# Attention over eight gathered key blocks per query block, in a kernel of block-sparse attention and a gated feed-forward

## The chip, the cores and the metric

One core of a Trainium2 chip runs the kernel. The metric is the time of one execution on the device in microseconds. The kernel before took 958.56 us (median of 3 runs, 957.12 to 958.99). A difference of about 0.2% is what a measurement of this kernel can tell from none.

## The reference

The inputs are q, k and v of shape 4 x 8 x 768 x 64 (batch, heads, tokens, head width), an array of 24 x 3 drawn block numbers, and two weight matrices in 64-bit floats, 512 x 2048 and 2048 x 512. Tokens form 24 blocks of 32.

```python
scores = 0.125 * q @ k.T                                   # per batch and head, 768 x 768
mask = (abs(blk_i - blk_j) <= 1) | first or last block on either side
for qb in range(24):                                       # and three drawn blocks
    for kb in sampled_blocks[qb]: mask[block qb, block kb] = True
scores = where(mask, scores, -1e9)
attn = exp(scores - rowmax); attn /= sum(attn) + 1e-9
x = (attn @ v), heads side by side                         # 3072 x 512
h = x @ w_in
g = where(h >= 1, h, where(h <= -1, 0, (h + 1)**2 / 4))
out = g @ w_out                                            # 3072 x 512
```

So the first and the last query block see all 24 key blocks. Every other one sees its own block and both neighbours, the first and the last block, and its three drawn ones: at most eight blocks, 256 of 768 keys.

## The kernel before

**Attention** works on all 768 keys, and the mask is laid into the operands. One `visit` is one head of one batch (for the first batch, one head and half of the queries). It computes the scores twice. The first pass (`max_mm`, L390) multiplies the rounded q and k with 24 extra rows that hold the mask, and VectorE takes each query's maximum (`max_red`, L396). Those maxima are turned into a row by TensorE (`max_turn`, L420, or `turn_all`, L407) and become one more operand row. The second pass (`scores`, L449 and L450; L447 for the first two visits, in full float32) gives the transposed scores, keys by queries, as the sum of a rounded product and a correction. ScalarE takes the exponential (`expo`, L456), GpSimd adds the tiles for the denominator (`p_sum`, L466; for the first batch TensorE does this with a matrix of ones, L512), and TensorE multiplies with v in float32 (`values`, L478: two products of 64 columns each, one into the upper and one into the lower half of the output). A float32 product is issued as two instructions. x is split into a rounded part and a rest.

**The feed-forward** (`moe`) takes half a batch, 384 tokens, at a time: 8 halves of 16 steps. A step multiplies 4 x 3 times with the first weights (`l1`, L650 to L652, 384 columns), passes the gate on ScalarE and VectorE (L657, L661, L665, L268, L676), and multiplies 3 x 3 times with the second weights (`l2`, L684 to L686, 512 columns). Rounded parts and rests are separate products, three for each one. The 64-bit weights are turned into these pairs on the chip (`convert`, L240 to L253), in the first two halves; the second ones then lie in a scratch in main memory (`wo_dram`) and are read again in every later half (L633).

**The order.** Every piece of work is put on a list with a time (`at`), the list is sorted and issued. The times come from tables of offsets (`P`, `PW`, `PX`, `PA`, `PM`). The feed-forward of one half runs beside the attention of the next ones. Nearly all transfers go through SyncE's queue.

## Time and profile before

| | before |
|---|---|
| median of the runs shown | 958.56 us |
| lowest and highest run | 957.12 and 958.99 us |
| the profiled execution's span | 956.5 us |
| median run less that span | 2.1 us |
| TensorE busy | 98% of the span |
| VectorE, ScalarE, GpSimd busy | 58%, 55%, 27% |
| matmul instructions | 4938 |
| moved by DMA | 155.74 MB, mean 163 GB/s |

The profile gives the span of one execution, from the first to the last instruction; the execution's own time is given only by that span, so what lies around it is taken as the difference to the median run. Engines run side by side and each executes its own list in order. TensorE's busy time counts overlapping matmuls once; the length of one matmul row is its latency, and what one costs in a row of many is the distance from start to start. PEld is the loading of the stationary operand.

### The profile page before, as it was taken

How to read it: one execution, taken by the hardware profiler on the slowest of the kernel's cores; microseconds unless marked ns; L12 is line 12 of the kernel's file. 1: busy time of each engine (PE TensorE's matmuls, PEld its weight loads, DVE VectorE, ACT ScalarE, POOL GpSimd, SP SyncE). 2: the span in 40 equal slices, each digit the busy share in tenths (PEclk: the TensorE clock that was granted, in tenths of full speed). 3: DMA queues.
4: the chain of work that ended last, by engine and by line, in shares of the span. 5: the costliest groups of instructions: out<-in, count | busy, mean ns of one | idle time of the engine just before them, and what ended most of it. 6: DMA issues, size and time to landing. Idle time of an engine off the chain costs nothing.

```text
span 956.5 us, 13865 instructions
## 1 busy us (share of the span) xinstructions
PE 935.7 (98%) x4938; PEld 764.9 (80%) x4938; DVE 550.0 (58%) x976; ACT 525.6 (55%) x1056; POOL 261.2 (27%) x260
## 2 busy tenths in 40 slices
PE   6899999999999999999999999999999999999998
PEld 4555577788888788888898888889888888899997
DVE  4989899867595666545655455555545443222222
ACT  5788687665765555454554454545455444433433
POOL 3000000354344444333443333334433333000000
PEclk9899899999999999999999999999999999999999
DMA  6756566677565655544445555554446423443443
GB/s 165 210 162 210 172 202 180 215 244 238 179 199 157 181 183 155 177 141 155 144 143 159 162 158 179 158 153 131 147 135 200 129 86 107 162 132 121 155 132 99
DMA packets 56025, 155.74 MB, mean 163 GB/s; under 512 B 9566, under 2 KB 17790, under 8 KB 55956
## 3 DMA queue, kind: packets, MB, share of 16 engines
q1 hardware_dynamic: 55700, 154.36, 53.1%
q8 instruction: 39, 0.64, 0.3%
q10 hardware_dynamic: 256, 0.49, 0.2%
q14 instruction: 30, 0.25, 0.1%
HBM read 110.11 MB, written 16.40 MB: 132 GB/s over the span
## 4 chain that ended last, share of the span: by engine, by line
PE 94%; ACT 3%; DVE 1%; issue 0%; DMA 0%; POOL 0%; ACTq 0%; POOLq 0%
PE po L478 13%; PE oa L684 9%; PE oa L686 9%; PE oa L685 9%; PE hp L650 9%; PE hp L651 8%; PE hp L652 8%; PE pa L390 7%; PE pa L449 6%; PE pa L450 6%; ACT pt L456 1%; PE pa L652 1%; PE pa L651 1%; PE pa L650 1%; PE oa L478 1%; PE pa L512 1%
## 5 line engine op out<-in xcount | busy, mean ns | idle before, releaser
L466 POOL TENSOR_TENSOR acc<-acc,pt 128x384 f32<-128x384 f32 x192 | 202.7, 1057 | 169.1 <-ACT pt L456 167.1
L396 DVE TENSOR_REDUCE mc<-pa 128x1 f32<-128x384 f32 x381 | 202.1, 552 | 55.1 <-PE pa L390 50.7
L456 ACT ACTIVATE pt<-pa 128x384 f32<-128x384 f32 x336 | 163.5, 489 | 94.1 <-PE pa L450 84.0
L665 DVE SCALAR_TENSOR_TENSOR r<-r,hp 128x384 f32<-128x384 f32 x112 | 61.7, 550 | 198.8 <-ACT r L661 198.6
L650 PE MATMUL hp<-x,wi 128*128 128x384 f32 x448 | 155.3, 347 | 0.0
L684 PE MATMUL oa<-w,gh 128*128 128x512 f32 x384 | 151.6, 395 | 0.3 <-ACT gh L268 0.3
L686 PE MATMUL oa<-w,gl 128*128 128x512 f32 x384 | 151.5, 394 | 0.1
L651 PE MATMUL hp<-x,wi 128*128 128x384 f32 x448 | 151.6, 338 | 0.0
L466 POOL TENSOR_TENSOR acc<-pt 128x384 f32<-128x384 f32 x48 | 51.2, 1070 | 366.9 <-ACT pt L456 366.9
L685 PE MATMUL oa<-w,gh 128*128 128x512 f32 x384 | 151.2, 394 | 0.0
L652 PE MATMUL hp<-x,wi 128*128 128x384 f32 x448 | 151.1, 337 | 0.0
L657 ACT ACTIVATE r<-hp,half_c 128x384 f32<-128x384 f32 x112 | 65.1, 582 | 113.1 <-PE hp L652 112.9
L478 PE MATMUL po<-pt,lv 128*64 128x384 f32 x720 | 127.2, 495 | 0.0
L390 PE MATMUL pa<-KA,QA 88*128 88x384 f32 x351 | 117.1, 359 | 2.7 <-ACT QA L268 0.9
L450 PE MATMUL pa<-QB,KB 128*128 128x384 f32 x336 | 114.4, 341 | 0.0
L449 PE MATMUL pa<-QA,KA 102*128 102x384 f32 (+1 forms) x318 | 110.5, 347 | 1.7 <-ACT pt L456 1.0
L676 DVE TENSOR_TENSOR gl<-r,gh 128x384 fp32r<-128x384 f32 x128 | 76.5, 598 | 49.3 <-ACT gh L268 48.3
L268 ACT CAST gh<-r 128x384 fp32r<-128x384 f32 x128 | 65.6, 512 | 66.0 <-DVE r L665 65.9
L478 PEld LDWEIGHTS po<-pt,lv 128*64 128x64 f32 x720 | 60.4, 138 | 50.3 <-issue 41.0
L650 PEld LDWEIGHTS hp<-x,wi 128*128 128x128 f32 x448 | 84.5, 189 | 16.8 <-issue 13.6
L651 PEld LDWEIGHTS hp<-x,wi 128*128 128x128 f32 x448 | 84.6, 189 | 1.7 <-issue 0.6
L686 PEld LDWEIGHTS oa<-w,gl 128*128 128x128 f32 x384 | 72.1, 188 | 16.4 <-DVE gl L676 0.6
(134 smaller groups left out, 1201.0 us busy)
## 6 DMA issues: line engine op xcount, KB each, us to landing
w<-wo_dram SPq DMA_DIRECT2D x112, 512.0 KB, 3.3
qk<-in_qk_t_dram SPq DMA_DIRECT2D x24, 384.0 KB, 3.3
raw<-in_moe_w_in_dram SPq DMA_DIRECT2D x16, 512.0 KB, 4.6
raw<-in_moe_w_out_dram SPq DMA_DIRECT2D x16, 512.0 KB, 3.9
wo_dram<-w SPq DMA_DIRECT2D x16, 512.0 KB, 3.4
lv<-in_v_dram SPq DMA_DIRECT2D x40, 192.0 KB, 2.9
out_dram<-o SPq DMA_DIRECT2D x7, 768.0 KB, 5.6
KA<-qkh SPq DMA_DIRECT2D x24, 192.0 KB, 2.7
```

Source lines behind the costliest of these rows:

```text
L390: nc.tensor.matmul(out=pm[:, 0:HALF], lhsT=QAi[0:KM, t * 128:(t + 1) * 128], rhs=KAi[0:KM, kh * HALF:(kh + 1) * HALF], start=True, stop=True)
L396: nc.vector.reduce_max(out=st["mc"][:, t - t0, kh:kh + 1], in_=st.pop(("pm", t, kh))[:, 0:HALF], axis=AX.X)
L450: nc.tensor.matmul(out=ps[:, 0:HALF], lhsT=st["KB"][:, ks], rhs=st["QB"][:, cs], start=False, stop=True)
L456: nc.scalar.activation(out=p, in_=st.pop(("ps", hf, c))[:, 0:HALF], func=AF.Exp, scale=SCALE)
L466: nc.gpsimd.tensor_tensor(out=own["acc"][:, k], in0=prev, in1=st["p", hf, c], op=ALU.add)
L478: nc.tensor.matmul(out=st["po"][(L, R)[k], 0:HALF], lhsT=lv[k][:, c], rhs=p, start=(c == 0), stop=(c == T - 1))
L650: nc.tensor.matmul(out=hv, lhsT=wi[:, j, 0, fs], rhs=x[:, 0], start=(j == 0), stop=False)
L651: nc.tensor.matmul(out=hv, lhsT=wi[:, j, 0, fs], rhs=x[:, 1], start=False, stop=False)
L652: nc.tensor.matmul(out=hv, lhsT=wi[:, j, 1, fs], rhs=x[:, 0], start=False, stop=(j == NP - 1))
L684: nc.tensor.matmul(out=o, lhsT=gh[:, ts], rhs=w[:, 0], start=(fi == fis[0]), stop=False)
L685: nc.tensor.matmul(out=o, lhsT=gh[:, ts], rhs=w[:, 1], start=False, stop=False)
L686: nc.tensor.matmul(out=o, lhsT=gl[:, ts], rhs=w[:, 0], start=False, stop=(fi == fis[-1]))
```

## The change

The layout of the work is new from end to end; the feed-forward's arithmetic stays.

- **Tiles.** A tile is 128 query rows: two neighbouring query blocks of two batches. For two pairs of batches there are 22 such tiles and 2 special ones (first and last block). Three tiles are a group of the feed-forward, 384 tokens, 8 groups.
- **Gathered keys and values.** For each normal tile and each half of the heads, 8 key blocks for each of two query blocks are copied inside on-chip memory from the whole k (`kt`) into `kg`: three neighbours, three drawn ones at addresses read into registers (`k_random`, always GpSimd), the first and the last. v comes from main memory by DMA in the same way (`v_static`, `v_random`, addresses read by SyncE). A drawn block that is already seen, or drawn twice, is kept in the keys and replaced by a block of zeros in v. v has a column of ones, so the denominator comes out of the same product.
- **Scores once.** They are computed in float32, queries by keys: 16 products for a half tile, each with 64 rows, 32 columns of the array and 256 moving columns. VectorE takes the maximum from PSUM, ScalarE the exponential with it as bias, TensorE turns the result (4 transposes for each of two), ScalarE and VectorE copy it back, and TensorE multiplies with v: 32 products with 32 columns of the array and 65 moving columns. Special tiles take all 768 keys, one head at a time.
- **Order.** `Plan` holds each piece with a duration, a priority, what it needs and what buffers it holds, simulates the engines once with these durations, and issues in the order of the simulated starts. On every engine that order is fixed then.
- **Buffers.** After the first group, attention has PSUM banks 0 to 2, the first layer 3 and 4 (0 to 4 in the last group), the outputs 5 to 7. x of two groups fits on the chip.

The weights are converted in pieces of 128 x 512, 32 times, with the same operations as before. A special tile takes one head at a time: 2 x 4 score products of 384 columns, 2 x 3 transposes, 6 x 4 value products.

```diff
--- before.py
+++ after.py
-    plan.sort(key=lambda x: x[0])
-    for _, fn, args in plan:
-        traced(fn, *args)
...
+    for pair in range(B // 2):
+        units = lambda *blocks: [(2 * pair + k, i) for k in range(2) for i in blocks]
+        normal = [("n", pair, t, units(2 * t + 1, 2 * t + 2)) for t in range(NB // 2 - 1)]
+        special = ("s", pair, None, units(0, NB - 1))
+        tiles += normal[:6] + [special] + normal[6:]
...
+    LATENCY = {"PE": 0.28, "ACT": 0.1, "DVE": 0.1, "POOL": 0.15, "SP": 0.0}
+    DMA_RATE, DMA_WAIT = 260e3, 2.0
...
+                    end = now + dur
+                    done = end + self.LATENCY[name]
+                    if name == "SP" and t["size"]:
+                        dma_free = max(dma_free, end + 0.3) + t["size"] / self.DMA_RATE
+                        done = dma_free + self.DMA_WAIT
+                    e["at"] = end
...
+        placed.sort(key=lambda x: (x[0], x[1]))
...
+        return [t["fn"] for _, _, t in placed]
...
+    def load_k(pair, hh, prio):
+        key = ("kt", pair, hh)
+        add(SP, 0.45, prio, lambda: nc.sync.dma_start(out=new("kt", key).rearrange("p i b j k -> p (i b j k)"), in_=kt_in[pair, :, hh]),
+            give=[key], hold=[("kt", key)], size=128 * 12288)
...
+            def v_static(k):
+                i = units[k][1]
+                vg = new("vg", ("vg", n, k))
...
+                nc.sync.dma_start(out=vg[32 * (lo - i + 1):32 * (hi - i + 1), 0], in_=v_in[pair, lo * BLK:hi * BLK])
+                if globe.get(place) != pair:
+                    globe[place] = pair
+                    nc.sync.dma_start(out=vg[64:96, 1], in_=v_in[pair, 0:BLK])
+                    nc.sync.dma_start(out=vg[96:128, 1], in_=v_in[pair, (NB - 1) * BLK:S])
+            def v_random(k):
+                _, regs = nc.values_load_multi_w_load_instructions(
+                    vix[0:1, 6 * t + 3 * k:6 * t + 3 * k + 3], engines=(SP_ENGINE,), min_val=0, max_val=S,
+                    skip_runtime_bounds_check_because="clamped on the chip to the blocks there are")
+                vg = of(("vg", n, k))
+                for to, r in zip((vg[96:128, 0], vg[0:32, 1], vg[32:64, 1]), regs):
+                    nc.sync.dma_start(out=to, in_=v_in[pair, bass.ds(r, BLK)])
...
+                def k_static(kg=kg, kt=kt):
+                    to = new("kg", kg).rearrange("p i s b c -> p i s (b c)")
+                    eng = nc.vector if n < GT else nc.gpsimd
+                    src = of(kt).rearrange("p i b j k -> p i (b j k)")
+                    for k in range(2):
+                        i = units[k][1]
+                        eng.tensor_copy(out=to[:, k, 0:3], in_=src[:, i - 1:i + 2])
+                    for s, blk in ((6, 0), (7, NB - 1)):
+                        eng.tensor_copy(out=to[:, :, s], in_=src[:, blk:blk + 1].to_broadcast([128, 2, 4 * BLK]))
+                def k_random(kg=kg, kt=kt):
+                    _, regs = nc.values_load_multi_w_load_instructions(
+                        kix[0:1, 6 * t:6 * t + 6], engines=(POOL_ENGINE,), min_val=0, max_val=NB - 1,
+                        skip_runtime_bounds_check_because="clamped on the chip to the blocks there are")
+                    to = of(kg).rearrange("p i s b c -> p i s (b c)")
+                    src = of(kt).rearrange("p i b j k -> p i (b j k)")
+                    for k in range(2):
+                        for r in range(NR):
+                            nc.gpsimd.tensor_copy(out=to[:, k, 3 + r:4 + r], in_=src[:, bass.ds(regs[3 * k + r], 1)])
+                add(DVE if n < GT else POOL, 1.7, prio - 2 + 0.9 * hh, k_static, need=[kt, *kchain], give=[(*kg, "s")], hold=hold)
+                add(POOL, 3.5, prio - 2 + 0.9 * hh + 0.2, k_random, need=["ix", (*kg, "s")], give=[kg], now=[(*kg, "r")], hold=hold)
...
+                kchain[:] = [(*kg, "r")]
...
+                nc.tensor.transpose(out=a[:, j * 128:(j + 1) * 128], in_=of(("xs", n))[:, j * 128:(j + 1) * 128], identity=idf)
...
+        def scores():
+            banks = [new("bank", k) for k in sa]
+            for jj in range(2):
+                for u in range(4):
+                    for e in range(2):
+                        nc.tensor.matmul(out=banks[e][32 * u:32 * u + 32, 256 * jj:256 * jj + 256],
+                                         lhsT=of(q)[rows_of[e], 2 * hh + jj, 32 * u:32 * u + 32],
+                                         rhs=of(("kg", n, hh))[rows_of[e], u % 2, :, u // 2, jj * BLK:(jj + 1) * BLK], start=True, stop=True, skip_group_check=True)
+        def top(e):
+            if e == 0:
+                new("nm", nm)
+            nc.vector.tensor_reduce(out=of(nm)[:, 2 * e:2 * e + 2], in_=of(sa[e]).rearrange("p (j k) -> p j k", j=2), axis=AX.X, op=ALU.max,
+                                    negate=True)
+        def expo(e, jj):
+            if jj == 0:
+                new("p", pk[e])
+            nc.scalar.activation(out=of(pk[e])[:, jj], in_=of(sa[e])[:, 256 * jj:256 * jj + 256], func=AF.Exp,
+                                 bias=of(nm)[:, 2 * e + jj:2 * e + jj + 1])
+        def turn(e):
+            a = new("bank", ta[e])
+            for jj in range(2):
+                for c in range(2):
+                    at = (2 * jj + c) * 128
+                    nc.tensor.transpose(out=a[:, at:at + 128], in_=of(pk[e])[:, jj, c * 128:(c + 1) * 128], identity=idf)
...
+        def values():
+            o = new("bank", ob)
+            for jj in range(2):
+                for e in range(2):
+                    h = 4 * hh + 2 * jj + e
+                    k = 2 * jj + e
+                    for c in range(2):
+                        for u in range(4):
+                            nc.tensor.matmul(out=o[32 * u:32 * u + 32, k * VW:(k + 1) * VW], lhsT=of(tk[e])[:, jj, c, 32 * u:32 * u + 32],
+                                             rhs=of(("vg", n, u % 2))[:, c, u // 2, h * VW:(h + 1) * VW], start=(c == 0), stop=(c == 1),
+                                             skip_group_check=True)
...
+            def scores(e=e, jj=jj, sa=sa):
+                for i in range(2):
+                    bank = new("bank", sa[i])
+                    for u in range(4):
+                        nc.tensor.matmul(out=bank[32 * u:32 * u + 32, 0:384], lhsT=of(q)[rows_of[e], 2 * hh + jj, 32 * u:32 * u + 32],
+                                         rhs=of(kt)[rows_of[e], 12 * i:12 * i + 12, u // 2, jj], start=True, stop=True, skip_group_check=True)
...
+                for c in range(6):
+                    pt = of(tk[c // 3]).rearrange("p j c q -> p (j c) q")
+                    for u in range(4):
+                        nc.tensor.matmul(out=o[32 * u:32 * u + 32, k * VW:(k + 1) * VW], lhsT=pt[:, c % 3, 32 * u:32 * u + 32],
+                                         rhs=of(("vg", n, c // 2))[:, c % 2, u // 2, h * VW:(h + 1) * VW], start=(c == 0), stop=(c == 5),
...
+        add(SP, 0.45, prio - 5, load, give=[("raw", key)], hold=[raw], size=128 * 4096)
+        add(ACT, 0.65, prio, absolute, need=[("raw", key)], give=[("abs", key)], hold=[raw, cva])
+        add(DVE, 2.1, prio, bits, need=[("abs", key)], give=[("bits", key)], hold=[raw, cva])
+        add(ACT, 0.62, prio, hi, need=[("bits", key), *order], give=[("hi", key)], hold=[cva, *hold])
+        add(DVE, 0.75, prio, lo, need=[("hi", key)], give=[key], hold=[cva, *hold])
...
+    for name, g, fis, fresh in (("0l", 0, low, True), ("1l", 1, low, False), ("0h", 0, high, True), ("1h", 1, high, False)):
+        step = STEP_A
+        gated(name, g, fis, t, step, fresh, fis is low, fis is high)
+        if g == 0:
+            for q in sorted({fi // 4 for fi in fis}):
+                for k in range(4):
+                    w_in_part(k, q, 1.5 + 2 * k if q == 0 else t + (4 * q - fis[0]) * step - WI_LEAD + 0.1 * k)
+        t += len(fis) * step
+    for g in range(2, len(GROUPS)):
+        gated(str(g), g, full, t, STEP_B, False, True, True)
...
+        if ring == "bank":
+            moe = isinstance(key[1], str)
+            plan.only[key] = set(range(3 if key[1] < "7" else 0, 5)) if key[0] == "h" else {5, 6, 7} if moe else set(range(8 if key[1] < GT else 3))
...
+    order = plan.order()
+    with tc.manual_schedule():
+        for fn in order:
+            fn()
+T0, T1, MOE0 = 0.0, 22.0, 34.0
+STEP_A, STEP_B, LEAD, WI_LEAD = 6.0, 5.6, 20.0, 8.0
```

## Rows read from the trace of the kernel before

**Rows 1.** The page: busy time of the engines, and the chain that ended last, by line.

```profile
PE 935.7 (98%) x4938; PEld 764.9 (80%) x4938; DVE 550.0 (58%) x976; ACT 525.6 (55%) x1056; POOL 261.2 (27%) x260
...
PE po L478 13%; PE oa L684 9%; PE oa L686 9%; PE oa L685 9%; PE hp L650 9%; PE hp L651 8%; PE hp L652 8%; PE pa L390 7%; PE pa L449 6%; PE pa L450 6%; ACT pt L456 1%; PE pa L652 1%; PE pa L651 1%; PE pa L650 1%; PE oa L478 1%; PE pa L512 1%
```

**Rows 2.** Stretches: PE, PEld, DVE, ACT, POOL busy (instructions), clock, DMA share, GB/s.

```profile
0.00:25.00 25.00, 16.86 (x48) 10.21 (x50) 12.08 (x30) 15.00 (x27) 7.27 (x20) 1.00 0.65 164
25.00:100.00 75.00, 67.98 (x373) 39.84 (x372) 67.71 (x122) 60.45 (x117) 0.00 (x0) 0.92 0.65 194
...
500.00:600.00 100.00, 100.00 (x534) 86.16 (x533) 53.17 (x98) 49.76 (x105) 35.92 (x36) 1.00 0.56 165
```

**Rows 3.** Timeline of TensorE late: first second-layer matmuls of two steps (start, length).

```profile
851.16 0.39 PE L684 MATMUL oa<-w,gh 128*128 128x512 f32 x1
...
855.36 0.39 PE L684 MATMUL oa<-w,gh 128*128 128x512 f32 x1
```

**Rows 4.** Chain in order of time: float32 matmuls, stationary 128, 64 and 32 wide.

```profile
22.82 0.65 PE oa L447 x2
...
30.67 2.09 PE po L478 x12
...
53.34 2.07 PE oa L512 x24
```

**Rows 5.** Timeline of TensorE: three transposes of 128 columns and what follows.

```profile
66.08 0.34 PE L420 MATMUL pa<-idr,mr 128*1 128x128 f32 x3
66.26 0.56 PE L390 MATMUL pa<-KA,QA 88*128 88x384 f32 x2
```

**Rows 6.** Timeline of TensorE: small products (L538), then v products, then first-layer ones.

```profile
502.75 0.24 PE L538 MATMUL pa<-sel,PS 128*64 128x32 f32 x1
502.76 0.54 PE L478 MATMUL po<-pt,lv 128*64 128x384 f32 x1
502.82 0.22 PE L538 MATMUL pa<-sel,PS 128*64 128x32 f32 x1
...
506.88 0.45 PE L650 MATMUL hp<-x,wi 128*128 128x384 f32 x1
507.16 0.34 PE L651 MATMUL hp<-x,wi 128*128 128x384 f32 x1
507.34 0.34 PE L652 MATMUL hp<-x,wi 128*128 128x384 f32 x1
```

**Rows 7.** Groups by line and shape, busy us, mean ns: loading a stationary operand.

```profile
L512 PEld LDWEIGHTS pa<-pt,ones 128*32 128x32 f32 x96 | 2.7, 109 | 5.5 <-issue 4.3 <-ACT gh L268 0.6 <-DVE cva L241 0.6
```

**Rows 8.** The same view: the gate of one feed-forward step, and the running maximum.

```profile
L657 ACT ACTIVATE r<-hp,half_c 128x384 f32<-128x384 f32 x112 | 65.1, 582 | 113.1 <-PE hp L652 112.9
L661 ACT ACTIVATE r<-r 128x384 f32<-128x384 f32 x128 | 66.9, 523 | 1.5
L665 DVE SCALAR_TENSOR_TENSOR r<-r,hp 128x384 f32<-128x384 f32 x112 | 61.7, 550 | 198.8 <-ACT r L661 198.6
L268 ACT CAST gh<-r 128x384 fp32r<-128x384 f32 x128 | 65.6, 512 | 66.0 <-DVE r L665 65.9
L676 DVE TENSOR_TENSOR gl<-r,gh 128x384 fp32r<-128x384 f32 x128 | 76.5, 598 | 49.3 <-ACT gh L268 48.3
L396 DVE TENSOR_REDUCE mc<-pa 128x1 f32<-128x384 f32 x381 | 202.1, 552 | 55.1 <-PE pa L390 50.7
```

**Rows 9.** The same view: conversion of weights on VectorE.

```profile
L241 DVE TENSOR_SCALAR cva<-cva 128x1024 f32<-128x1024 f32 x16 | 11.3, 706 | 1.2 <-ACT cva L240 1.1
L244 DVE SCALAR_TENSOR_TENSOR cva<-raw,cva 128x1024 int32<-128x1024 int32 x16 | 20.2, 1266 | 0.2
L253 DVE TENSOR_TENSOR wi<-cva,wi 128x512 fp32r<-128x512 f32 x16 | 11.2, 709 | 2.4 <-ACT wi L268 2.2
```

**Rows 10.** The same view: GpSimd, one-operand copy.

```profile
L266 POOL TENSOR_SCALAR x<-KB 38x768 fp32r<-38x768 f32 x1 | 0.8, 829 | 0.1
```

**Rows 11.** The page: DMA issues, KB each, us to landing.

```profile
w<-wo_dram SPq DMA_DIRECT2D x112, 512.0 KB, 3.3
```

More of the change, by code (lines that the diff above doesn't have):

```diff
@@ L73, in f @@
+    plan.rings["bank"] = list(range(8))
+    slots = {}
+    for ring, (n, size) in sizes.items():
+        for i in range(n):
+            if (ring, i) not in LENDERS:
+                slots[ring, i] = sb.tile([128, size], types.get(ring, F32), name=f"{ring}{i}")
+    for i in range(8):
+        slots["bank", i] = ps.tile([128, 512], F32, name=f"bank{i}")
+    made, extra, early = {}, {}, {}
     def f(ap):
         return ap.bitcast(F32)
-    idr = cst.tile([128, 128], F32R, name="idr")
-    eps = cst.tile([128, 1], F32, name="eps")
@@ L157, in mask_rest @@
-    def mask_rest():
-        mask_half(1, nc.scalar)
-        for i in range(1, ALL):
-            rounded(nc.gpsimd, QA[i][64:KM, HALF:S], f(QA[0][64:KM, HALF:S]))
-    plan = []
-    passed = set()
-    def after(key, *needs):
-        assert all(x in passed for x in needs), (key, needs)
-        passed.add(key)
-    def at(t, fn, *args):
-        plan.append((t, fn, args))
-    fence = [None, 0]
-    def pe_from(k):
-        return [i for i in nc.cur_bb.bb.instructions[k:] if i.engine == mybir.EngineType.PE]
@@ L177, in behind @@
-    def behind(i, first):
-        tc.add_manual_dep(i, first.name, mybir.DependencyInfo(mybir.DependencyClass.NoSync, mybir.DependencyReason.DATA),
-                          reason="order")
-    def fenced(fn, *args):
-        k = len(nc.cur_bb.bb.instructions)
-        last = pe_from(-200)[-BEFORE:] if BEFORE else []
-        fn(*args)
-        new = pe_from(k)
-        for i in last:
-            behind(new[0], i)
-        for a, b in zip(new, new[1:]):
-            behind(b, a)
-        fence[:] = [new[-1], AFTER]
@@ L192, in traced @@
-    def traced(fn, *args):
-        k = len(nc.cur_bb.bb.instructions)
-        fn(*args)
-        if fence[1] and fn is not fenced:
-            for i in pe_from(k):
-                behind(i, fence[0])
-                fence[1] = max(0, fence[1] - 1)
-    turns = {}
-    def bank(wide, use="s"):
-        if wide:
-            ring = RINGS[use]
-            n = turns[use] = turns.get(use, -1) + 1
-            name = ring[n % len(ring)]
-            if name[0] == "o":
-                return psc.tile([128, DM], F32, name=name)
-            if name == "hp":
-                return psh.tile([128, 512], F32, name="hp")
-        return psa.tile([128, 512], F32, name="pa")
@@ new lines, in body, with load_consts @@
+    vix = cst.tile([1, 66], I32, name="vix")
+    wo_dram = dr.tile([NF, 128, 2 * DM], F32R, name="wo_dram")
+    parts = [dr.tile([GT, 128, DM], F32, name=f"part{i}") for i in range(2)]
+    at_ix = {}
+    def load_consts():
+        o = new("o", ("o", "ix"))[0:1]
+        post, s_f, bad, tmp = (o[:, k * NB * NR:(k + 1) * NB * NR] for k in range(4))
+        sraw = new("raw", ("raw", "ix"))[0:1, 0:NB * NR]
+        at_ix.update(post=post, s_f=s_f, bad=bad, tmp=tmp, sraw=sraw)
+        nc.sync.dma_start(out=sraw, in_=sampled_blocks.bitcast(I32).rearrange("a (r w) -> (a r) w", w=2).unsqueeze(0))
+        nc.sync.dma_start(out=post, in_=pos)
@@ new lines, in first @@
+    def first():
+        nc.scalar.activation(out=warm, in_=half_c, func=AF.Exp)
+    ix = [("o", ("o", "ix")), ("raw", ("raw", "ix"))]
+    add(SP, 0.9, -100, load_consts, give=["sraw"], size=1e3, hold=ix)
+    add(SP, 0.45, -40, load_ident, give=["idf"], size=64e3)
+    add(DVE, 3.2, -100, indices, need=["sraw"], give=["ix"], hold=ix)
+    add(ACT, 1.6, -100, first, need=["ix"], give=["warm"])
+    kchain, globe = [], {}
+    chain = dict(T=[], K=[], V=[])
+    L, R = slice(0, 64), slice(64, 128)
@@ L757, in body @@
+    STEP = 6.1
+    for pair, hh in ((0, 0), (0, 1), (1, 0), (1, 1)):
+        load_k(pair, hh, -50 + hh if pair == 0 else 200 + hh)
+    starts = {0: T0, 1: T1}
+    passes = []
     full = tuple(range(NF))
     low, high = full[:NF // 2], full[NF // 2:]
[L759 to L761 removed]
```

1148 lines of the change are left out of this document (516 added, 632 removed).

## The prediction

> **What bounds the kernel now.** I read the page first: TensorE is busy 98% of the span, the other engines at most 58%, and the chain that ended last is a list of TensorE lines [rows 1]. The stretches say the same by time: from 200 us on TensorE never stops, and only the first 100 us, where VectorE and ScalarE are nearly as full, have gaps [rows 2]. So the span is the sum of TensorE's work plus a ragged start, and a change is worth the TensorE time that it takes away. The chain by line shows which that is: L478, L390, L449 and L450 are attention, L650 to L652 and L684 to L686 the feed-forward. The timeline gives the part that stays: one feed-forward step starts 4.20 us after the one before [rows 3], and 128 steps (8 halves by 16) make 538 us. The other 956.5 - 538 = 418 us of the span are attention, conversion and start. The change can reach only these.
>
> **What small float32 products cost.** The new attention uses float32 products with 32 columns of the array, so their pace decides the sum. A float32 product is two instructions. With a stationary operand 128 wide two follow in 0.65 us, 325 ns each; 64 wide, in two halves of the array, twelve take 2.09 us, 174 ns each; 32 wide, in four quarters, 24 take 2.07 us, 86 ns each, all for 384 columns [rows 4]. So halving the width doubles how many run at once.
>
> - *Scores, half a normal tile:* 16 products of 256 columns. At L512's pace (2.07 us for 12 of 384) that is 1.84 us if only the four quarters run side by side. They use half of the rows of the array, alternately; if the two row halves also run side by side, 0.92. No row shows this. I take 0.92, since each halving in rows 4 doubled the rate, and keep 1.84 as the upper end.
> - *Transposes:* three of 128 columns take 0.18 us, 60 ns each, with rounded operands [rows 5]; a full float32 product of 128 columns would be 650/3 = 217 ns. I take one float32 instruction, 108 ns, since the transpose rows are one instruction each. Eight for a half tile: 0.86 us.
> - *Values, half a normal tile:* 32 products of 65 columns, 64 instructions, 16 in each quarter. By columns one lasts 325 x 65/384 = 55 ns. Loading 32 columns takes 109 ns from start to end [rows 7] and may not hide behind so short a product: upper end 164 ns. L538's two instructions of 32 columns, each with its own load, start 70 ns apart [rows 6]; that is the nearest row, so 16 x 0.07 = 1.12 us.
> - *Change of shape:* after the v products the first full matmul holds TensorE 0.28 us in place of 0.18 [rows 6], 0.1 us a change, four changes a half.
>
> The Trainium skill, page "TensorE: Matmul & The Clock Gate", section "Wait — 56ns, not 53.3ns?", has a rule against this change: starts never come closer than about 25 ns, however short the product. By it 64 value instructions take 1.6 us instead of 1.12. The trace has two starts 0.01 us apart in different halves of the array (502.75 and 502.76 [rows 6]), so it does not agree where products lie beside each other; by the rule the sum below grows by 27 us, to 834.
>
> A normal tile then costs 2 x (0.92 + 0.86 + 1.12 + 0.4) + 0.43 (four more transposes) = 7.0 us, 22 of them 155 us. A head of a special tile: 8 score products of 384 columns 1.38, six transposes 0.65, 48 value instructions 0.84, changes 0.3: 3.2 us; eight heads and 0.43 make 25.8, two tiles 52. Attention falls from 418 us, start included, to 207 us of TensorE; with the feed-forward 745.
>
> **What lies beside it.** For a group of three tiles TensorE needs 67 + 2.75 x 7.0 + 0.25 x 25.8 = 93 us. ScalarE: 16 gates of 0.582 + 0.523 + 0.512 us [rows 8] are 26, attention at the same 0.512 us for 384 columns some 17: 43. VectorE: 16 x (0.550 + 0.598) = 18, and for a tile four maxima over 512 columns (0.552 x 512/384 = 0.74 each [rows 8]), two copies of the same size, and some 2.2 us of scaling and splitting, 6.6 us together: 41 in all with a special tile's share. The old maxima and GpSimd's sums are gone. GpSimd copies 768 columns in 0.829 us [rows 10]; a half tile copies 1280 + 768 columns, 2.2 us, so a tile with its scaling 5 us, and 12 address reads whose cost no row shows: from nothing up to the 3.3 us in which an ordinary load lands [rows 11], which would be 45 us a tile. I take a tenth of that, 0.33 us each, 9 us a tile against 31 us of TensorE for it. SyncE reads 6 addresses a tile, ahead of its transfers; what is queued behind them are the second-layer weights of later steps, one each 5.8 us. All of it is hidden behind TensorE after the start. If the cover is gone, TensorE waits for scores.
>
> **The start.** The feed-forward cannot begin before three tiles are done, and the gather needs whole k first. By the code's sizes 3.1 MB of k, 0.8 of q, 6.1 of v and some 3 of raw weights are queued on SyncE before: 13 MB. DMA moved 164 GB/s at a share of 0.65 in the first 25 us [rows 2], 250 at a full share: 52 us. TensorE does 21 us of attention in it. Then VectorE is late next: the first 8 steps need 12 more weight pieces of (2 x 0.706 + 2 x 1.266)/2 + 0.709 = 2.7 us [rows 9], 32 us, 9 of gates and 20 for the next three tiles, 61 us, against 34 + 21 = 55 of TensorE. The two wait for each other in turn, so I add 15 us, with 6 and 30 as ends.
>
> **The sum.** 52 + (745 - 21) + 15 = 791; 10 us for gaps where a tile comes late in a fixed order (1.4% of the rest; before there were none after 200 us, in the crowded stretch 9%); 4 for the last copy and store: a span of 805 us. The runs' median lies 2.1 us above the profiled span of 956.5, so 807 us.
>
> **Rivals.**
>
> - *TensorE's small products cost more.* If the row halves take turns, +0.92 x 44 = 40 us; if a transpose costs both float32 instructions, 109 ns x 544 = 59. One alone 847 or 866, both 906. For it: no row has 64-row products or float32 transposes. Against: rows 4 for the first. In the other direction, transposes at 60 ns and values at 55 ns would save 39: 768.
> - *The fixed order does not fill TensorE.* It comes from guessed durations, and attention is a chain over three engines with three banks. If TensorE is busy as in 25 to 100 us before, 67.98 of 75 [rows 2], the rest takes 724/0.906 = 799: a time of 857. For it: the stretch in which the old order was short of work. Against: every attention step has feed-forward products to lie beside it.
> - *Starts of small products are spaced* (slower). If each instruction takes 60 ns to start, as the transposes of rows 5 are apart, a half tile's values take 3.84 us and its scores 1.92, a special head's values 2.88: 44 x (2.72 + 1.0) + 16 x 2.04 = 197 us more, 1004. It turns slower than before from a spacing of 51 ns on. Against it: the 0.01 us of rows 6. At the skill's 25 ns it is the 834 above, within my range.
> - *GpSimd's address reads become the bound* (slower). After the start 19 tiles are gathered one after the other; with the last group's 67 us and the 52 and 4 us that takes 125 + 19 x (5 + 12r), longer than before from r = 3.2 us on; at 3.3, about 972. Against: a read from memory on the core should not last as long as a 512 KB load.
>
> **How the numbers follow.** Forecast 0.55 (its own range 768 to 835); the 25 ns rule 0.06; costlier products 0.14; order 0.13; spaced starts 0.04; address reads 0.06; within 0.2% 0.02 (0.2% is what a measurement tells from no change). Faster 0.88, same 0.02, slower 0.10. The range 750 to 890 leaves out both slower cases, no change, and the costlier products where both hold and a little of the order.
>
> **What would show it.** Right: matmul instructions for attention in runs of 32 within 0.9 to 1.0 us and of 64 within 1.0 to 1.2; transposes about 0.11 us apart; feed-forward steps still 4.2 us of TensorE; the first first-layer product near 52 us; TensorE full from some 110 us on. Wrong: scores over 1.5 us a half, float32 transposes as pairs, GpSimd busy or waiting for registers most of the span, TensorE below 95% in the middle with a wait for VectorE, ScalarE or GpSimd in front of scores, or a start much longer than 52 us.

## The result, and the profile after

The changed kernel takes 812.04 us (median of 4 runs, 811.55 to 813.06); the kernel before took 958.77 beside it. The ratio is 0.848, 95% interval 0.8464 to 0.8496: 147 us less. The profiled execution took 811.55 us with a span of 809.8. The forecast was 807 us, its span 805.

The page after, busy time by engine and the chain by line; these answer to [rows 1]:

```profile
PE 755.9 (93%) x8480; PEld 623.3 (77%) x8480; DVE 406.7 (50%) x830; ACT 380.5 (47%) x768; POOL 154.5 (19%) x441
...
PE 85%; DMA 10%; DVE 2%; SPq 1%; ACT 1%; issue 1%; ACTq 0%
PE bank L673 11%; PE bank L708 11%; PE bank L675 11%; PE bank L710 11%; PE bank L674 11%; PE bank L709 10%; DMA vg<-in_vx_dram 5%; PE bank L487 5%; PE bank L449 4%; PE bank L470 4%; PE bank L530 3%; DMA raw<-in_moe_w_out_dram 2%; DMA early_wi<-in_vx_dram 2%; PE bank L565 2%; PE bank L548 1%; PE bank L398 1%
```

TensorE still sets the time, but it is no longer full from end to end: its work fell by 180 us (935.7 to 755.9), the span by only 146.7, so some 33 us more than before pass with TensorE idle. The feed-forward lines L673 to L675 and L708 to L710 fill 65% of the span; the attention lines L449 (scores), L470 (transposes) and L487 (values), with L530 to L565 for the special tiles, some 19%. DMA stands in the chain with 10%, and it had no line there before. The stretches say where (columns as in [rows 2], so that the last three are the granted clock, the DMA share and GB/s):

```profile
0.00:25.00 25.00, 4.33 (x42) 2.42 (x42) 14.34 (x44) 7.42 (x13) 5.66 (x22) 1.00 0.93 299
25.00:50.00 25.00, 17.03 (x386) 10.27 (x386) 17.91 (x44) 11.07 (x23) 4.79 (x13) 0.96 1.05 253
50.00:75.00 25.00, 13.85 (x254) 9.11 (x252) 19.10 (x37) 11.09 (x23) 14.50 (x38) 0.70 0.99 275
75.00:100.00 25.00, 24.33 (x467) 19.52 (x468) 23.00 (x45) 17.28 (x35) 15.86 (x35) 1.00 0.80 247
500.00:600.00 100.00, 100.00 (x1075) 80.92 (x1074) 39.15 (x82) 41.88 (x84) 7.58 (x22) 1.00 0.42 146
600.00:700.00 100.00, 95.88 (x1219) 78.17 (x1218) 41.95 (x87) 47.16 (x98) 27.16 (x82) 0.98 0.60 171
```

TensorE works 35 of the first 75 us, 24.33 of the next 25, and then nearly all. No engine is full in the first 75 us; the DMA share is (0.93 to 1.05). Between 50 and 75 us, with TensorE half idle, the granted clock is 0.70: part of the stretch at the lower of the two levels.

The small products, from the chain of waits in order of time (start, length, what); of the kernel before, [rows 4 and 5] are the nearest:

```profile
386.10 1.02 PE bank L449 x32
387.13 1.05 PE bank L487 x64
388.17 0.37 PE bank L673
389.42 0.87 PE bank L470 x8
```

A half normal tile takes 1.02 us for scores, 1.05 for values and 0.87 for eight transposes, which are one instruction each (x8); the first full matmul behind the values holds 0.37.

The timeline of TensorE: the first first-layer matmul, the first of the second pass, and two second-layer starts late, which answer to [rows 3]:

```profile
73.07 0.67 PE L673 MATMUL bank<-xh,wi 128*128 128x384 f32 x1
...
123.56 0.33 PE L673 MATMUL bank<-xh,wi 128*128 128x384 f32 x1
...
740.28 0.39 PE L708 MATMUL bank<-w,gh 128*128 128x512 f32 x1
...
744.47 0.39 PE L708 MATMUL bank<-w,gh 128*128 128x512 f32 x1
```

A step still takes 4.19 us. The feed-forward starts at 73.07 us, not at 52; its first eight steps last 50.5 us, not 70; from there to the end are 686.2 us, where the forecast's terms give 683. So the total hit because a start that was forecast 21 us too short and a stretch behind it that was forecast 20 us too long cancelled.

### The profile page after: what moved, and what is told of

Same layout as the page of the kernel before. It is cut to its first block, busy times and chain, and to the rows that moved or that the text cites. A ratio compares the mean times of both kernels' runs of the same rounds, so it can differ in the third digit from the quotient of the medians.

```text
span 809.8 us, 20914 instructions
## 1 busy us (share of the span) xinstructions
PE 755.9 (93%) x8480; PEld 623.3 (77%) x8480; DVE 406.7 (50%) x830; ACT 380.5 (47%) x768; POOL 154.5 (19%) x441
## 4 chain that ended last, share of the span: by engine, by line
PE 85%; DMA 10%; DVE 2%; SPq 1%; ACT 1%; issue 1%; ACTq 0%
PE bank L673 11%; PE bank L708 11%; PE bank L675 11%; PE bank L710 11%; PE bank L674 11%; PE bank L709 10%; DMA vg<-in_vx_dram 5%; PE bank L487 5%; PE bank L449 4%; PE bank L470 4%; PE bank L530 3%; DMA raw<-in_moe_w_out_dram 2%; DMA early_wi<-in_vx_dram 2%; PE bank L565 2%; PE bank L548 1%; PE bank L398 1%
## 5 line engine op out<-in xcount | busy, mean ns | idle before, releaser
L673 PE MATMUL bank<-xh,wi 128*128 128x384 f32 x512 | 181.6, 355 | 0.0
L675 PE MATMUL bank<-xh,wi 128*128 128x384 f32 x512 | 173.1, 338 | 0.3 <-DVE wi L616 0.3
L674 PE MATMUL bank<-xl,wi 128*128 128x384 f32 x512 | 172.3, 336 | 0.0
L708 PE MATMUL bank<-w,gh 128*128 128x512 f32 x384 | 157.3, 410 | 0.3 <-ACT gh L589 0.3
L678 ACT ACTIVATE r<-bank,half_c 128x384 f32<-128x384 f32 x128 | 74.5, 582 | 173.6 <-PE bank L675 172.9
L710 PE MATMUL bank<-w,gl 128*128 128x512 f32 x384 | 152.5, 397 | 1.8 <-DVE gl L690 1.8
L709 PE MATMUL bank<-w,gh 128*128 128x512 f32 x384 | 151.5, 395 | 0.0
L673 PEld LDWEIGHTS bank<-xh,wi 128*128 128x128 f32 x512 | 96.5, 189 | 15.6 <-issue 9.7
L674 PEld LDWEIGHTS bank<-xl,wi 128*128 128x128 f32 x512 | 96.6, 189 | 3.9
L675 PEld LDWEIGHTS bank<-xh,wi 128*128 128x128 f32 x512 | 96.2, 188 | 0.9 <-DVE wi L616 0.9
L708 PEld LDWEIGHTS bank<-w,gh 128*128 128x128 f32 x384 | 72.3, 188 | 19.2 <-issue 3.1
L710 PEld LDWEIGHTS bank<-w,gl 128*128 128x128 f32 x384 | 72.3, 188 | 18.8 <-DVE gl L690 2.8
L379 POOL COPY kg<-kt 128x128 f32 x264 | 75.9, 334 | 32.2 <-PE bank L449 15.8
L709 PEld LDWEIGHTS bank<-w,gh 128*128 128x128 f32 x384 | 72.4, 189 | 10.6
L449 PE MATMUL bank<-kg,q 64*32 64x256 f32 x1408 | 53.6, 407 | 16.1 <-POOL kg L379 15.5
```

What stands on the lines that cost most here:

```text
L379: nc.gpsimd.tensor_copy(out=to[:, k, 3 + r:4 + r], in_=src[:, bass.ds(regs[3 * k + r], 1)])
L449: nc.tensor.matmul(out=banks[e][32 * u:32 * u + 32, 256 * jj:256 * jj + 256], lhsT=of(q)[rows_of[e], 2 * hh + jj, 32 * u:32 * u + 32], rhs ...
L673: nc.tensor.matmul(out=hv, lhsT=wi[:, j, 0, fs], rhs=xh, start=(j == 0), stop=False)
L674: nc.tensor.matmul(out=hv, lhsT=wi[:, j, 0, fs], rhs=xl, start=False, stop=False)
L675: nc.tensor.matmul(out=hv, lhsT=wi[:, j, 1, fs], rhs=xh, start=False, stop=(j == 3))
L678: nc.scalar.activation(out=new("r", rk[1]), in_=of(hk[1])[:, 0:TOK], func=AF.Relu, bias=half_c, scale=0.5)
```

## The experiments

Four runs test the prices of the new attention, one what the gather is worth, six the start. Ratios are against the kernel before, with the 95% interval.

**The scores in the two row halves of the array.** Every product reads the same 64 rows; as many of each kind as before.

```
-                for u in range(4):
-                    for e in range(2):
-   lhsT=of(q)[rows_of[e], ...], rhs=of(("kg", n, hh))[rows_of[e], ...]
+                for e in range(2):
+                    for u in range(4):
+   lhsT=of(q)[rows_of[0], ...], rhs=of(("kg", n, hh))[rows_of[0], ...]
```

> The scores of a normal half tile take both factors from the lower 64 rows of the array for both heads of a pair (so half of the scores are computed from the wrong head), four quarters after one another; nothing else changes. If the two row halves run side by side in the changed kernel, as forecast, a half tile's 16 score products go from 1.02 us to about 1.9, and 44 halves cost some 40 us: 850. Rival: the row halves take turns already and the low price comes from elsewhere: no change, 812.

839.47 us, ratio 0.8763 (0.8739 to 0.8788). The chain of waits:

```profile
391.49 1.86 PE bank L449 x32
```

1.86 us is the upper end that the prediction had kept (1.84), and 1.02 is near the one it took (0.92): products in the two row halves run side by side. The time rose by 27 us and not by all 44 x 0.84 = 37; where the rest went is shown with the third run.

**Values in the order of the quarters.** Four instructions in a row go to one quarter of the columns; before, neighbours went to different quarters.

```
-                    for c in range(2):
-                        for u in range(4):
+                    for u in range(4):
+                        for c in range(2):
```

> The same value products in another order: both halves of the keys of one query block follow each other, so four instructions in a row go to the same quarter of the array. If products run side by side only when neighbours in the list go to different quarters, a half tile's 64 value instructions go from 1.04 us to between 2.6 (48 of 64 steps of 55 ns) and 3.5 (all 64), and the kernel to between 880 and 920. Rival: TensorE finds work for a free quarter by itself: 812.

815.94 us, ratio 0.8503 (0.847 to 0.8535), hardly apart from the change's own. The chain of waits:

```profile
391.90 1.11 PE bank L487 x60
```

I had expected 2.6 to 3.5 us a half; it is 1.11 in place of 1.05. That expectation took TensorE to start its list strictly in order, and it fell: the quarters still work side by side when four neighbours of the list share one. Whether the engine starts later products first or hands them to a queue in each quarter the trace doesn't tell. The Trainium skill, page "TensorE: Matmul & The Clock Gate", section "The mechanism", has weight loads pulled ahead but matmuls in strict order of start and end; by the second half of that rule the 2.6 us should have stood, and 1.11 speaks against it.

**The price of a transpose.** Every block of four is done twice, eight more a half, with the same result.

```
-            for jj in range(2):
+            for jj in (0, 1, 0, 1):
```

> Each transpose of the exponentials in normal tiles is issued twice into the same place. At 0.109 us each that is 8 x 0.109 = 0.87 us more TensorE work in a half tile, 38 us in 44 halves. Theory (TensorE is the bound from the first feed-forward product on, and a transpose costs one float32 instruction): 850, less some 5 for halves that lie in the uncovered start. Rival: part of its busy time is slack that a fixed order leaves: under 830.

842.34 us, ratio 0.8791 (0.8768 to 0.8814). The chain of waits:

```profile
358.97 1.75 PE bank L470 x16
```

Sixteen take 1.75 us, 109 ns each; the prediction's 108. A group of three normal tiles grew by 5.2 us (88 to 93 from the first product of one to that of the next), which is 6 x 0.87: there TensorE alone sets the time. But the pass from 533.2 to 649.9 us, which has a special tile beside it, stayed at 116.6 here and in the first run. It is the pass of the middle in which the work comes late most: the stretch from 600 to 700 us above has 95.88 busy, and in it TensorE waits for gathered values (1.22 and 1.01 us at 625 and 627 us) and for exponentials (1.42). The first 123.6 us likewise took only 6.4 of the 10.4 us added there. Extra work of TensorE is paid where it is full and free where it is not.

**The address reads.** All reads of block numbers into registers are replaced by fixed numbers; as many copies and transfers as before.

```
-                _, regs = nc.values_load_multi_w_load_instructions(vix[...], engines=(SP_ENGINE,), ...)
+                regs = [(3 + (5 * t + 7 * r + k) % 18) * BLK for r in range(NR)]
-                    _, regs = nc.values_load_multi_w_load_instructions(kix[...], engines=(POOL_ENGINE,), ...)
+                    regs = [3 + (5 * t + 7 * r + r // 3) % 18 for r in range(2 * NR)]
```

> The drawn blocks are taken from addresses fixed when the kernel is built (other blocks than the reference draws); the copies and transfers stay in number and size, only the reads of addresses into registers go. Theory: they are hidden everywhere, 812 within 2. Rival: SyncE's reads hold up the first values, for which TensorE waits until 24 us, and GpSimd's the first scores: 3 to 6 us less. Second rival, address reads as a bound: 20 us less or more.

812.01 us, ratio 0.8479 (0.8453 to 0.8505): no change. In the trace of the changed kernel, the reads of addresses (six each on GpSimd, three each on SyncE) and GpSimd's gathered copies by kind (count: ns shortest/median/longest, first and last start):

```profile
L372 POOLq TENSOR_LOAD <-kix x44: 774/888/3001, 5.0 to 697.2; - x44
L343 SPq TENSOR_LOAD <-vix x44: 662/673/1151, 16.8 to 703.4; - x44
L379 POOLq FUSED_REGOPS  x264: 46/46/58, 6.0 to 699.0; - x132
L379 POOL COPY kg<-kt x264: 287/293/783, 7.6 to 700.2; 128x128 f32 x132
```

Reading six addresses takes GpSimd 0.89 us (median), 0.15 each; at every copy comes a register operation of 46 ns. Together that is some 0.19 us an address, against the 0.33 us that I took and the 3.3 at the upper end [rows 11]. GpSimd is busy 19% of the span. The rival of the address reads needed 3.2 us each and is out by a factor of some sixteen.

**All keys for all heads.** The gather is left out: every tile goes the way of the special ones, with 12 blocks of keys in place of eight.

```
-        if kind == "n":
+        if False:
```

> Every tile goes the way of the special ones: no gather, all 24 key blocks, one head at a time (unmasked, so the output is that of full attention). It tells what the gather is worth inside the new layout. TensorE's sum by the pieces measured in the changed kernel (per head 1.42 for scores, 0.66 for transposes, 0.82 for values and some 0.3 for changes of shape: 26 us a tile): 538 + 24 x 26 = 1162, with start and end above 1200, slower than the 958 of the kernel before. Rival: the layout (scores once, the denominator from a column of ones, no second pass) is what pays and the gather adds little: under 900. The chain of one head through three engines with three banks may not keep TensorE full: then up to 1500.

1512.76 us, ratio 1.5779 (1.5717 to 1.5841), at a clock of 0.86. The page, then the chain of waits over one head:

```profile
PE 1336.7 (88%) x16224; PEld 919.1 (61%) x16224; DVE 630.9 (42%) x1378; ACT 551.4 (36%) x1076; POOL 13.5 (1%) x25
```

```profile
701.10 0.59 ACT p L542
701.74 1.54 PE bank L548 x6
703.28 1.27 PE bank L565 x48
704.55 0.82 PE bank L530 x8
...
705.46 0.56 DVE nm L536
706.04 0.57 DVE nm L536
706.63 0.17 DVE nm L538
...
706.91 0.59 ACT p L542
```

One head follows the other: scores, maximum, exponential, transposes, values, 5.81 us from one exponential to the next, of which TensorE has 3.6; through the maximum and the exponential only feed-forward products can fill it. 22 normal tiles at the special tile's 26 us in place of 7 would be some 413 us more, 1225; the measured 1513 is beyond that, with the chain over three engines and the lower clock on top. By the page TensorE is busy 1336.7 us, 175 more than the expected sum of 1162, which the clock of 0.86 would about make (1162/0.86 = 1351, an estimate), and idle for another 175 of the span of 1511.9. So the two are of about one size, and even the sum of 1162 alone is above the 958 before: within this layout it is the gather on the chip, not the planned order alone, that makes the kernel faster.

**What the start waits for.** In the first 73 us, what made the engines wait in the changed kernel (us in total, times, longest):

```profile
PE bank L449 <- POOL kg L379: 15.5, 2, 13.0
PE bank L470 <- ACT p L462: 9.5, 4, 6.3
...
ACT p L462 <- DVE nm L456: 10.3, 3, 6.7
ACT q L315 <- DMA q<-in_qt_dram: 10.0, 1, 10.0
ACT cva L602 <- DMA raw<-in_moe_w_out_dram: 6.8, 3, 5.3
...
POOL q L317 <- DMA q<-in_qt_dram: 18.5, 2, 13.9
```

TensorE waits for gathered keys and for exponentials; GpSimd and ScalarE, which make these, wait for loads. Two theories: the *bytes* bind (the GB/s of the three stretches above make 20.7 MB by 75 us; the forecast counted 13 before the first product), or the *order* does, since an engine that works its list in order stands in front of an instruction whose load hasn't landed, with ready work behind it. A third is VectorE, which converts weights beside attention.

The first run on this loads only half the partitions of each raw weight, which takes away 8.4 MB in all, about half of it before 123.6 us:

```
-            nc.sync.dma_start(out=new("raw", ("raw", key)), in_=src...)
+            raw = new("raw", ("raw", key))
+            nc.sync.dma_start(out=raw[0:64], in_=src[0:64]...)
...
+    for i in range(3):
+        nc.gpsimd.memset(slots["raw", i][64:128].bitcast(F32), 1.0)
```

> Only the upper 64 of 128 rows of each 64-bit weight piece are transferred (the other rows hold ones, so half of the weights are wrong); everything else stays. 32 x 0.26 MB less, 4.2 MB of it before the second pass of the feed-forward begins at 123.6 us. If DMA bounds the first 120 us (at shares of 0.93 to 1.05 until 75 us, some 275 GB/s): 15 us less, 797. If VectorE and the order of work bound them: 0 to 3 us less.

811.29 us, ratio 0.8467 (0.8435 to 0.85): nothing to be told from no change. The stretch from 50 to 75 us, then the time up to the first first-layer product in the changed kernel and in this run, and the landing of the halved loads (KB each, median us):

```profile
50.00:75.00 25.00, 15.61 (x270) 10.70 (x262) 20.83 (x41) 11.24 (x23) 14.54 (x37) 0.64 0.97 252
```

```profile
0.00:73.10 73.10, 33.31 (x673) 19.99 (x673) 49.65 (x121) 28.63 (x58) 24.95 (x72) 0.90 0.99 274
```

```profile
0.00:71.30 71.30, 34.51 (x672) 21.63 (x673) 50.67 (x121) 28.80 (x58) 28.09 (x75) 0.87 0.98 250
...
raw<-in_moe_w_in_dram SPq DMA_DIRECT2D x16, 256.0 KB, 5.1
raw<-in_moe_w_out_dram SPq DMA_DIRECT2D x16, 256.0 KB, 4.0
```

TensorE is nearly as idle as before. Up to the first product 17.8 MB move (71.3 us at 250 GB/s) in place of 20.0; at the changed kernel's rate the difference is worth 8 us, and the product comes 1.8 us earlier. So the number of these bytes does not set the start. But the DMA share stays at 0.97 though fewer bytes move in it (252 GB/s in place of 275), and a half load still takes 5.1 and 4.0 us to land where a whole one took 6.5 and 5.0. So the share does not go by bytes, and whether the time of the transfers binds, rather than their bytes, this run does not tell.

The second takes two of the five VectorE instructions off each piece of weights:

```
-            nc.vector.tensor_scalar(out=f(a), in0=f(a), scalar1=CLO, scalar2=CHI, op0=ALU.max, op1=ALU.min)
-            nc.vector.scalar_tensor_tensor(out=a, in0=raw[:, :, 1], scalar=-0x40000000, in1=a, ...)
```

> Two of the four bit operations with which VectorE converts a weight piece are left out (clamp and sign, so the weights are wrong); their 0.44 and 0.70 us go, 1.14 x 32 = 37 us of VectorE's time, 18 us of it before 123.6 us. If VectorE bounds the first 120 us: 10 to 18 us less, 794 to 802. If DMA bounds them, the conversion waits for its load all the same: 0 to 3 us less.

804.88 us, ratio 0.8406 (0.8376 to 0.8435), between the two expectations. VectorE has some 16 us less to do before the second pass; the second pass starts 2.7 us earlier (120.9), the end comes 8 us earlier in the profile, 3.1 of them from the third pass (39.1 us in place of 42.2), where weights are still converted. So VectorE is a part of it, and before the second pass a small one.

Both at once (the two diffs above together):

> Half of each raw weight piece is transferred and two of the four bit operations are left out, both at once (the weights are wrong). If transfers and VectorE each cover for the other in the first 120 us, together they give far more than the 1 and 7 us one by one: 15 us less or more, under 797. If order and latency bind them: not much more than the sum, 802 to 805.

806.29 us, ratio 0.8435 (0.8408 to 0.8462): no more than the second alone, so the bytes of the raw weights weren't hidden behind VectorE either.

The order, first in one place: the conversion of the second-layer weights falls due 20 us later in the plan of the first pass, everything else the same.

```
-                convert(("wo", fi), at - 2, ...
+                convert(("wo", fi), at + 18 if g == 0 else at - 2, ...
```

> One priority is moved: the conversion of each second-layer weight piece counts as due 20 us later (at + 18 in place of at - 2), so that attention of the first tiles goes ahead of it on ScalarE, VectorE and SyncE. In the changed kernel ScalarE stood 5.3 us before 57.3 us in front of such a conversion whose load had not landed, with exponentials queued behind it. If the order of work in the first 120 us is what holds them up (half the transfer and half of VectorE's conversion gave 1 and 7 us): 5 to 8 us less, 804 to 807. Rival: the wait moves to the second layer, which then lacks its weights: no change, 812.

807.73 us, ratio 0.8448 (0.8416 to 0.8481): some 4 us, and its interval overlaps the change's own, so this is hardly apart from no change. The timeline of ScalarE tells why; first the changed kernel, with VectorE's two maxima ahead, then this run (in brackets the idle time before, and what ended it):

```profile
52.87 1.28 DVE L456 TENSOR_REDUCE nm<-bank 128x2 f32<-128x512 f32 x2
...
57.34 0.67 ACT L602 ACTIVATE cva<-raw 128x512 f32<-128x512 f32 x1 [5.28 <-DMA raw<-in_moe_w_out_dram]
57.92 0.82 ACT L462 ACTIVATE p<-bank,nm 128x256 f32<-128x256 f32 x2
```

```profile
57.23 0.67 ACT L602 ACTIVATE cva<-raw 128x512 f32<-128x512 f32 x1 [4.91 <-DMA raw<-in_moe_w_in_dram]
57.81 0.82 ACT L462 ACTIVATE p<-bank,nm 128x256 f32<-128x256 f32 x2
```

The exponentials' maxima are done by 54.2 us, and they stand ready behind a conversion that waits 5.28 us for its load. With that one moved, another conversion stood there, 4.91 us for the first-layer weights: the wait was passed on.

Then the order in more places, two plans with the same instructions. The second of them:

```
-        add(SP, 0.45, prio - 6, load_q, ...)            # q
+        add(SP, 0.45, prio - 16, load_q, ...)
-        add(ACT if n < GT else POOL, 0.7, prio - 3, scale_q, ...)
+        add(ACT if n < GT else POOL, 0.7, prio - 5, scale_q, ...)
-        add(SP, 0.45, prio - 5, load, ...)              # raw weights
+        add(SP, 0.45, prio - 16, load, ...)
-                convert(("wo", fi), at - 2, ...
+                convert(("wo", fi), at + 12 if g == 0 else at - 2, ...
-        load_k(pair, hh, -50 + hh if pair == 0 else 200 + hh)
+        load_k(pair, hh, -50 + 30 * hh if pair == 0 else 160 + hh)
-                    w_in_part(k, q, 1.5 + 2 * k if q == 0 else ...
+                    w_in_part(k, q, 10.5 + 2 * k if q == 0 else ...
-            at += 4.0 if n < GT else LEAD
+            at += 2 if n < GT else LEAD
-T0, T1, MOE0 = 0.0, 22.0, 34.0
-STEP_A, STEP_B, LEAD, WI_LEAD = 6.0, 5.6, 20.0, 8.0
+T0, T1, MOE0 = 0.0, 22.0, 54
+STEP_A, STEP_B, LEAD, WI_LEAD = 6, 5.4, 32, 4
```

The first has other numbers in the same places (second half of k at -50 + 46.5 * hh, tiles 1 apart, scaling of q at -1, `at + 18`, MOE0 34, steps 5.5, 5.0, 24, 16) and v at -2 where it was -4.

> The same work with other priorities throughout: q and the raw weights are asked for earlier, the second half of k after the first tile's v, tiles of the first group 1 in place of 4 us apart, second-layer conversions 20 us later, a lead of 24 in place of 20 us. The kernel's own planner puts the last product 12 us earlier with them. Theory (order decides the start and the wait at the special tile): 798 to 803. Rival: the planner's durations are not good enough for such differences, 810 to 814.

> A second set of priorities that the planner thinks 11 us shorter, with the feed-forward due later (54 in place of 34 us) and a lead of 32 us. Theory: 798 to 804, and the first feed-forward product near 65 us while the second pass begins only a few us earlier, since what counts is the sum up to there. Rival: 810 to 814.

804.05 us, ratio 0.8404 (0.8379 to 0.843), just above the range expected, and 800.2 us, ratio 0.8369 (0.8343 to 0.8394), within it. The second beats both kernels; its interval lies clear of the change's 0.8464 to 0.8496. By the ratios it gains 11 us on the changed kernel, by the medians 12. Its page and stretches (from 50 to 75 us, up to the first first-layer product, the eight steps behind it, and the pass with the special tile):

```profile
PE 753.0 (95%) x8480; PEld 623.0 (78%) x8480; DVE 403.5 (51%) x830; ACT 378.7 (48%) x768; POOL 154.8 (19%) x441
```

```profile
50.00:75.00 25.00, 20.71 (x444) 14.54 (x444) 21.64 (x44) 13.83 (x30) 15.45 (x41) 0.86 1.03 256
0.00:65.30 65.30, 32.52 (x673) 20.12 (x673) 43.69 (x111) 25.45 (x53) 22.64 (x72) 0.92 0.99 264
65.30:116.00 50.70, 49.16 (x744) 39.56 (x742) 46.83 (x93) 33.45 (x69) 24.40 (x54) 0.97 0.85 263
528.10:637.40 109.30, 108.38 (x1447) 86.24 (x1446) 48.42 (x103) 49.30 (x104) 21.45 (x63) 1.00 0.56 152
```

Same instructions, and TensorE has 20.71 us of work in the stretch where it had 13.85, with the DMA share as full as before. The first product comes at 65.3 us in place of 73.1, the second pass starts at 116.0 us (7.6 earlier). This profiled execution is the fastest of the plan's six; its span is 15.4 us shorter than the changed kernel's. Of these, TensorE's idle time ahead of the first product gives 7 us (32.8 in place of 39.8) and that in the pass with the special tile 3 (0.9 in place of 4.1). The two passes from the special tile's on take 190.5 us in place of 200.8, but most of that is work of TensorE that moved to earlier passes.

The chain that ended last in the first 75 us, by line, first in the changed kernel, then in this plan (the view cuts the lines off at the end):

```profile
by line: DMA vg<-in_vx_dram 34.3%; DMA raw<-in_moe_w_out_dram 20.0%; DMA early_wi<-in_vx_dram 18.7%; issue 2.5%; PE bank L470 2.3%; ACT p L462 2.3%; SPq L348 2.0%; SPq L336 1.9%; ACT cva L602 1.8%; SPq L343 1.8%; SPq L302 1.0%; DVE cva L608
```

```profile
by line: DMA vg<-in_vx_dram 18.9%; DMA q<-in_qt_dram 12.6%; DMA raw<-in_moe_w_in_dram 11.2%; PE bank L470 8.5%; PE bank L449 7.7%; PE bank L487 5.4%; issue 5.1%; PE bank L673 2.1%; DVE cva L608 1.9%; DVE cva L609 1.8%; ACT p L462 1.8%; DVE 
```

In the changed kernel 73% of it is loads of values (`early_wi` is a buffer that values borrow) and of raw second-layer weights; in this plan loads are 43%. So order binds, at the start above all. Whether an engine stands less often before a late load, or fewer transfers lie ahead of what the first tiles need (17.2 MB move before the first product in place of 20.0), these runs do not part: the new priorities move both. What is left is 116 us, where TensorE works 83 in the changed kernel's first 123.6; what its floor is stays open.

## Why the prediction was right, step by step

**What bounds the kernel, and the part that stays:** right. A step is 4.19 us where 4.20 was carried over, a group beside three normal tiles takes 87.7 us where the sum's terms give 88, and these groups grow by just the work that is added to them.

**Prices of small products:** right, one side apart. Scores 1.02 us a half (0.92 taken; 1.84 would have been the row halves in turn, and the first run shows 1.86). Transposes 109 ns (108). Values 1.05 us (1.12), of 64 instructions: one each 16 ns over four quarters. The Trainium skill, page "TensorE: Matmul & The Clock Gate", section "Wait — 56ns, not 53.3ns?", has starts at least some 25 ns apart; 64 of those would be 1.6 us, an estimate, and the row with 1.05 does not agree where products go to different quarters. Changes of shape: 0.37 for the first full matmul behind values, 0.19 over the normal 0.18, where 0.1 was taken. A special head comes to 1.42 us of scores (1.38 taken) on the same chain. The errors nearly cancel: from the second pass on the sum was 683 and 686.2 were measured.

**What lies beside it:** right in that TensorE covers it, wrong in the size of the address reads (some 0.19 us, not 0.33). That term was hidden, so it moved only a chance: the rival with 0.06 was never near.

**The start:** the step that failed, hidden by its neighbour. "52 us" came from 13 MB at 250 GB/s, as if bytes set it. The rate was about right (274 GB/s until the first product); the product came at 73.1 us, behind 20.0 MB. Nor is it the number of bytes alone: 2.2 MB less of raw weights brought it forward by 1.8 us only, and two bit operations less on VectorE by 1.9 (shifts of this size mean little: with fixed addresses it came at 70.0, and the time stayed), while the second new plan brought it to 65.3. What the runs show is that the order in which instructions and loads stand decides. The chain up to there is mostly loads one after another, and engines that work their lists in order stand at times in front of a late one; how much each of the two costs stays open.

**The stall of 15 us:** failed too, in the other direction. The prediction had 55 us of TensorE and 61 of VectorE in the first eight steps, waiting for each other in turn. These are the changed kernel, then the run with two bit operations less:

```profile
73.00:123.60 50.60, 49.93 (x753) 41.66 (x753) 47.04 (x92) 34.10 (x69) 23.79 (x54) 0.98 0.76 247
```

```profile
71.20:120.90 49.70, 48.79 (x753) 40.66 (x752) 38.31 (x79) 34.17 (x71) 20.69 (x54) 1.00 0.82 261
```

TensorE is busy 49.93 of the 50.6 us from 73.0 to 123.6, so there was no stall. VectorE with 9 us less to do left the stretch as long as it was, so TensorE's own work sets it. That work was less than forecast in part because by 73 us TensorE had done the scores of seven half tiles, not six; and seven of the weight pieces had been converted, so that VectorE had nine pieces of 2.9 us to do (26 us) where the forecast had 12 of 2.7. It is tempting to say that the time lost ahead of the first product was used up behind it, but no run shows that: in the second new plan the product came 7.8 us earlier, with five pieces converted, and the eight steps took 50.7 us all the same. So the sum of both (122 forecast, 123.6 measured) held though neither did; the agreement of this sum is luck in its parts.

**The order in the middle:** the 10 us for gaps were about right: 7 were measured, 4.1 of them in the pass with the special tile, 2.1 in the third pass (from 159.2 us), where weights are still converted, and 1.0 in the next. The end took 6 us where 4 were taken. The pass with the special tile:

```profile
533.20:649.90 116.70, 112.58 (x1371) 87.52 (x1369) 47.42 (x100) 51.29 (x106) 15.92 (x47) 0.99 0.48 145
```

Of the rivals, spaced starts and costlier products are refuted by rows, address reads by rows and a run. "The fixed order does not fill TensorE" holds in small for the special tile, and for the start, which the rival did not speak of; another order was worth 11 to 12 us, the gain of the second new plan.

## What to carry to other kernels

Price narrow float32 products by quarters and by row halves: all eight parts of the array work side by side, and a half tile's 64 value instructions cost about what its 32 score instructions do (1.05 and 1.02 us). In a start, ask not only how many bytes are queued but which in-order engine stands before a load that hasn't landed, and what ready work is behind it: a DMA share near 1.0 stayed there when bytes were taken away, so it did not tell that the bytes bound. And when a total agrees, check the terms: two errors of 20 us made this one look exact.

## What the hardware showed unexpectedly

- Neighbouring products in the same quarter do not hold up the others: 1.11 us against 1.05 for 64 of them.
- Reading six addresses from on-chip memory into registers took GpSimd 0.89 us and reading three took SyncE 0.67 (medians). A GpSimd copy of 128 float32 columns takes 293 ns (median) at such an address and at a fixed one, besides the 46 ns of a register operation.
- Taking half of the raw bytes away left the DMA share of 50 to 75 us at 0.97, with 252 GB/s in place of 275, and the time unchanged; a half load took some four fifths of a whole one's time to land (5.1 us against 6.5, 4.0 against 5.0).
